# Class 0 of a dilated neighbourhood attention kernel: two half steps of eight rows in place of one step of sixteen

## The chip, the cores and the metric

The kernel runs on one core of a Trainium2 chip. The metric is the device time of one execution in microseconds (us). The core has five engines that run their own instruction queues in order: TensorE (PE in the profile, with its weight loads as PEld), VectorE (DVE), ScalarE (ACT), GpSimd (POOL) and SyncE (SP, which here only issues transfers). They meet at semaphores.

## What is computed

The input is an image of 224 x 224 pixels with 192 channels. Every pixel attends to 7 x 7 pixels around it, taken two apart, so a pixel sees only pixels of one row parity and one column parity. At the border the window is moved inwards, not cut.

```python
qkv = x @ wqkv                       # q, k, v of 192 channels each, one head
r0 = clip(ir - 6, 0, 223 - 12)       # first row of the window; columns likewise
ri = r0[:, None] + 2 * arange(7)     # its seven rows
logits = einsum('bnc,bnkc->bnk', q, k[window]) * 192 ** -0.5
o = einsum('bnk,bnkc->bnc', softmax(logits), v[window]) @ wo
```

## The kernel before

**Row classes.** Rows are put in two classes by the parity of the rows that they look at: class 0 looks at even rows, class 1 at odd ones. Each class has 112 query rows `v`. Class 0 holds the image rows 1, 3, 5 (moved in at the top border) and then 0, 2, 4, ...; class 1 holds 7, 9, ..., 223 and then 218, 220, 222. Query row `v` of class 0 needs the key rows `v-6` to `v` of its class (clipped at 0); row `v` of class 1 needs `v` to `v+6`. Columns are classed and shifted in the same way (`cc` 0 and 1), in 14 slots of 8 columns.

**Bands.** The image is loaded transposed (channels on partitions) in 14 bands of 16 image rows, eight rows of each class. A band is three transposing loads on the SP queue: channels 0 to 127 of the even columns to `XA[0]`, of the odd ones to `XA[1]`, and a middle part to `X1[b]` (two buffers). `xb_items` copies the middle part into `XB` (two copies of 64 x 1792 a band), and `sort_items` puts 8 x 8 pixel blocks next to one another in `XS` (three copies a band and class). Both run on POOL, those of the first bands on DVE. `XA` and `XB` hold six bands. The other 64 partitions of `XB` hold one-hot marks for row and column, which mask keys that lie outside a query's window; `marks` and `marks_on` spread them over the bands.

**Steps, pairs, jobs.** A step is 16 query rows of one class; the 14 steps take the classes in turn (`steps`). A job is one slot of a step: 16 rows x 8 columns = 128 queries. In TensorE the two row halves of a job (`h`) stand side by side, each with 64 weight columns. Two jobs make a pair, so a step is seven pairs. For pair `k` the loop issues `stage1` (scores, row maximum on DVE as `nmx`) and `stage1b` (exp on ACT as `p`); for pair `k-1` `stage2` (transposes of `p`, copied to `pt_sb`); for pair `k-2` `stage3` (`o_ps`) and `stage4` (division by the row sum, and the output transfers). Class 0's rows 0 to 7 have only eight key rows; in step 0 `key_rows` fills their window up with six masked ones.

**Work for the next step.** During a step, the pieces of the next one are made between the pairs (`w128`, `w64`). `g_items` gives the queries multiplied by the folded weights, in four groups of slots with three items each: two `whole` items, and one `halves` item that goes from PSUM to `gx` on ACT and then to `G` in two copies on POOL. `v_item` gives the values of one block of 16 key rows (`pv`, then `VF`); `vd_low` and `vd_high` copy halves of `VF` to `VD`, so that a row half finds its 16 key rows there in order. Step 0 makes its own values as well as those of step 1.

**Order.** `in_order` ties every engine to the program's order, so each queue is the order in which the Python code issues. POOL's copies go through a list, `pool_q`, of which up to four entries are issued after each pair. It also carries the output transfers of slot 0 (10 to 20 small ones per step), because the border columns go to odd places.

```python
steps = [(ti, rc) for ti in range(7) for rc in range(2)]
J.p = PP[J.rc][J.k % 2]
add = {0: sort_items(1, 1, pool), 1: sort_items(2, 1, pool), 3: sort_items(2, 0, pool), 5: xb_items(3, pool) + sort_items(3, 0, pool)}.get(m, [])
pool_q[:0] = add
pool_do(4)
```

Of the kernel before, what the change touches and what calls it, by code (L numbers as in the profile page):

```python
# [22 lines left out]
NSTEP = 14  # L23
# [33 lines left out]
def _rows(rc, ti):  # L57

    return [_phys(rc, 16 * ti + j) for j in range(16)]


def _runs8(rc, ti, h):

    return [(j0, nj) for (j0, nj, _r, _s) in _aff_runs(_rows(rc, ti)[8 * h:8 * h + 8])]
# [34 lines left out]
def kernel(  # L99
# [42 lines left out]
    for t in SS:  # L142
        nc.vector.memset(_win(t, 0, 128, 0, [[256, 2], [16, 14], [1, 2]]), NEG)

    def load_items(b):

        src = xp[16 * b:16 * b + 16].rearrange("r j c -> (r j) c")
        at = (16 * b) % (2 * RP) * S

        def one(k):  # L150
            if k == 1:
                X1[b] = x1_p.tile([128, BND], BF, name=f"x1_{b}", tag="x1")
            dst = X1[b][:] if k == 1 else XA[k // 2][:, at:at + BND]
            nc.sync.dma_start_transpose(out=dst.unsqueeze(1), in_=src[:, 128 * k:128 * k + 128])

        return [lambda k=k: one(k) for k in ((0, 2, 1) if b in (0, 2, 3) else (1, 0, 2))]
# [10 lines left out]
    def sort_items(b, rc, eng):  # L167

        hf = (b + rc) % 2
        return [lambda k=k: eng(out=_win(XS[rc], 0, 128, k * NSLOT * 128 + 64 * hf, [[128, NSLOT], [8, 8], [1, 8]]), in_=strip_in(b, rc, k))  # L170
                for k in (0, 2, 1)]
# [69 lines left out]
    for m in range(2):  # L241
        marks(m, 0, MM, nc.vector.tensor_copy)
    marks(0, MM, 2 * MM, nc.vector.tensor_copy)
# [3 lines left out]

    def g_col(rc, ti, s0, ns, eng):
        for cc in range(2):
            p = XCOL[cc]  # L250
            if s0 == 0:
                for h in range(2):
                    for (j0, nj) in _runs8(rc, ti, h):
# [4 lines left out]
    def g_row(rc, ti, s0, ns, eng, parts):  # L258

        for cc in range(2):  # L260
            p = XROW[cc]
            for (j0, nj, e0, estep) in parts:
                if s0 == 0:
                    for h in range(2):
                        for (r0, nr) in _runs8(rc, ti, h):
# [20 lines left out]
    g_col(0, 0, 0, 1, nc.scalar.copy)  # L286
# [14 lines left out]
    for rc in range(2):  # L301
        for t in PP[rc]:
            nc.gpsimd.memset(_win(t, 0, 128, 112 * rc, [[128, 8], [1, 16]]), 0.0)
# [32 lines left out]
    def v_mms(pv, at):  # L336
        for cc in range(2):
            for pas in range(2):
                for h in range(2):
# [17 lines left out]

    def v_first(j):
        def emit(dve):
            pv = ps_g.tile([128, 512], F32, name="pv", tag="pg")  # L360
            v_mms(pv, lambda k, h: _win(XS[1], 0, 128, k * NSLOT * 128 + 128 * j + 64 * h, [[1, 64]]))
# [3 lines left out]
    def first_sort(eng):  # L365
        return [lambda k=k: eng(out=_win(XS[1], 0, 128, k * NSLOT * 128, [[64, NSLOT], [8, 8], [1, 8]]), in_=strip_in(0, 1, k)) for k in (0, 2, 1)]  # L366
# [6 lines left out]
    def row_runs(rc, ti):  # L373

        runs = []
        for j, p in enumerate(_rows(rc, ti)):
# [23 lines left out]

    def g_items(rc, ti, s0, ns):
        rows = row_runs(rc, ti)
        w = 8 * ns

# [18 lines left out]
        def put(dst, off, pg, dve, p0=0, pn=128):  # L423

            a, m = s0, ns
            if s0 == 0:
                rr = [_runs8(rc, ti, h) for h in range(2)]
                if len(rr[0]) == len(rr[1]):
                    evac(_win(dst, p0, pn, off, [[64, 2], [8, 8], [1, 8]]), _win(pg, p0, pn, 0, [[8 * w, 2], [1, 8], [w, 8]]), dve)
                else:  # L430
                    for h in range(2):
# [3 lines left out]
            evac(_win(dst, p0, pn, off + (a - s0) * 128, [[8, 16], [128, m], [1, 8]]), _win(pg, p0, pn, 8 * (a - s0), [[w, 16], [8, m], [1, 8]]), dve)  # L435
# [8 lines left out]
        def halves(dve, direct=False):  # L444
# [9 lines left out]
            for cc in range(2):  # L454
                p = XDAT[cc]
                nc.gpsimd.tensor_copy(out=G[rc][cc][p:p + 64, 1, s0:s0 + ns, :], in_=gx[p:p + 64, 0:ns * 128].rearrange("p (s q) -> p s q", q=128))  # L456

        return [whole(0), whole(1), halves]

# [4 lines left out]
    def key_rows(J, h):  # L464

        i = 2 * J.ti + h
        if J.rc == 0:
            if i == 0:
                return [(MM - 6, 0, 6), (0, 6, 8)]
            v0 = 8 * i - 6  # L470
        else:
            v0 = 8 * i
        return [(v, v - v0, n) for (v, n) in _wraps(v0, 14)]

    def stage1(J, ab):
        s = 2 * J.m + ab
        s_ps = SS[ab]


        cols = {0: [(1, 7, S - 7), (8, 8, 0)], 2: [(1, 15, 9)]}.get(s, [(2, 14, 8 * s - 6)])  # L480
        lo = cols[0][0]
        for cc in range(2):
            units = []
            for h in range(2):
                u = []
                for (v, k0, n) in key_rows(J, h):
                    for (q, nq, c) in cols:
                        o = _win(s_ps, 64 * h, 64, cc * 256 + 16 * k0 + q, [[16, n], [1, nq]])
# [10 lines left out]
        nc.vector.tensor_reduce(out=nmx[:], in_=_win(s_ps, 0, 128, lo, [[256, 2], [16, 14], [1, 16 - lo]]), axis=AX.XY, op=ALU.max, negate=True)  # L499
        J.p = PP[J.rc][J.k % 2]  # L500
        J.s[ab] = (s_ps, nmx)

    def stage1b(J, ab):
        s_ps, nmx = J.s[ab]
        z = 16 if J.rc == 0 else 0
        for cc in range(2):
            nc.scalar.activation(out=J.p[:, ab, cc, :, z:z + 112].rearrange("p q (r k) -> p q r k", k=8), in_=_win(s_ps, 0, 128, cc * 256, [[8, 2], [16, 14], [1, 8]]),  # L507
                                 func=ACTF.Exp, bias=nmx[:, cc:cc + 1], scale=1.0)

    def stage2(J):  # L510
        J.pt = work.tile([128, 8, 128], BF, name="pt_sb", tag="pt_sb")
        if J.k == NP - 1:

            for ab in range(2):
                pt_ps = ps_g.tile([128, 4, 128], BF, name="pt_ps", tag="pg")
                for i in range(4):
                    for h in range(2):
                        nc.tensor.transpose(pt_ps[64 * h:64 * h + 64, i, :], J.p[:, ab, i // 2, i % 2, 64 * h:64 * h + 64], ident[:])
                nc.vector.tensor_copy(out=J.pt[:, 4 * ab:4 * ab + 4, :], in_=pt_ps[:])
            return  # L520
        pt_ps = ps_t.tile([128, 8, 128], BF, name="pt_ps", tag="pt")
        for ab in range(2):
            for cc in range(2):
                for q in range(2):
                    for h in range(2):
                        nc.tensor.transpose(pt_ps[64 * h:64 * h + 64, 4 * ab + 2 * cc + q, :], J.p[:, ab, cc, q, 64 * h:64 * h + 64], ident[:])  # L526
        (nc.scalar.copy if J.n == NSTEP - 1 and J.m < 5 else nc.vector.tensor_copy)(out=J.pt[:], in_=pt_ps[:])  # L527

    def stage3(J, ab):
        rc, s = J.rc, 2 * J.m + ab  # L530
        o_ps = (ps_o if J.k < NP - 1 else ps_g).tile([128, 512], F32, name="o_ps", tag="o" if J.k < NP - 1 else "pg")
        V = (VD[rc], VF[rc])
        for cc in range(2):
            for q in range(2):
                for h in range(2):
                    nc.tensor.matmul(o_ps[64 * h:64 * h + 64, cc * 193:cc * 193 + 193], lhsT=J.pt[:, 4 * ab + 2 * cc + q, 64 * h:64 * h + 64],  # L536
                                     rhs=V[h][:, (s - 1 + q) % NSLOT, cc * C:cc * C + 193], start=(q == 0), stop=(q == 1))
# [7 lines left out]
    def stage4(J, ab):  # L545
        rc, ti, s, o_ps = J.rc, J.ti, 2 * J.m + ab, J.o_ps[ab]
        rs = J.rs.get(ab) or stage4a(J, ab)
        if s > 0 and J.n == NSTEP - 1:

            o_sb = _win(XS[0], 0, 128, 2 * C * s, [[C, 2], [1, C]])  # L550
# [4 lines left out]
        if J.k >= NP - 3 and ab == 1:  # L555
# [5 lines left out]
        prow = _rows(rc, ti)  # L561
        if s > 0:
            for (j0, nj, r0, rstep) in _aff_runs(prow):
                def put(eng, j0=j0, nj=nj, r0=r0, rstep=rstep):
                    eng.dma_start(out=op[r0: r0 + (nj - 1) * rstep + 1: rstep, 8 * s - 3:8 * s + 5, :],
                                  in_=o_sb[8 * j0:8 * (j0 + nj)].rearrange("p t c -> p (t c)"))

                if J.n < NSTEP - 1:
                    put(nc.gpsimd if nj < 8 and s % 2 == 1 else nc.sync)
                elif nj >= 8:  # L570
                    put(nc.sync)
                elif s in SHORT:

                    for j in range(nj):
                        def row(eng, p=8 * (j0 + j), r=r0 + j * rstep, a=SHORT[s]):
                            eng.dma_start(out=op[r, 8 * a - 3:8 * s + 5, :].rearrange("(t i) c -> i t c", i=8),
                                          in_=_win(XS[0], p, 8, 2 * C * a, [[2 * C, s + 1 - a], [1, 2 * C]]))
                        if s < NSLOT - 1:
                            row(nc.gpsimd)
                        else:  # L580
                            end_q.append(row)
            return
        for h in range(2):
            for (j0, nj, r0, rstep) in _aff_runs(prow[8 * h:8 * h + 8]):
                for (cc, i0, n, mem, pair) in ((0, 0, 3, 1, 0), (0, 3, 5, 0, 0), (1, 6, 2, 1, 3), (1, 0, 3, 1, 109), (1, 3, 3, 0, 109)):
                    p = 64 * h + 8 * j0 + i0 * nj
                    dst = op[r0: r0 + (nj - 1) * rstep + 1: rstep, pair:pair + n, mem * C:(mem + 1) * C]
                    pool_q.append(lambda dst=dst, p=p, m=n * nj, cc=cc: nc.gpsimd.dma_start(out=dst.rearrange("j i c -> i j c"), in_=o_sb[p:p + m, cc, :]))  # L588

    steps = [(ti, rc) for ti in range(7) for rc in range(2)]  # L590
    pairs = []
    for n, (ti, rc) in enumerate(steps):
        for m in range(7):
            J = Pair()
            J.n, J.ti, J.rc, J.m, J.k, J.o_ps, J.s, J.rs = n, ti, rc, m, len(pairs), {}, {}, {}
# [3 lines left out]
    def g_all(n):  # L599
        ti, rc = steps[n]  # L600
        its = [g_items(rc, ti, s0, ns) for (s0, ns) in GROUPS]
# [4 lines left out]
    end_q = []  # L606
    SHORT = {7: 1, NSLOT - 1: 8}
# [4 lines left out]


    first0, first1 = ((0, 6, 0, 0), (6, 10, 0, 1)), ((0, 16, 0, 1),)
    g_row(0, 0, 0, 1, pool, first0)
    g_col(0, 0, 1, 3, pool)
# [159 lines left out]
```

## Time and profile before

| what | value |
|---|---|
| median of 3 runs | 362.85 us (362.56 to 364.27) |
| profiled execution, its own time | 360.51 us |
| its span | 358.7 us |
| busy PE, DVE, ACT, POOL | 93%, 88%, 86%, 79% of the span |
| step 0, first exp to first exp of step 1 | 37.46 us |
| step 1; step 2 | 23.37 us; 24.46 us |
| steps 3 to 12 | 226.64 us, 22.7 each |
| step 13 and what follows | 25.20 us |

The profiled execution is 2.34 us below the median. The steps are told apart by the first exp (`p`) of each, of which there are 28 a step. [...]

### The profile page before, as it was taken

To read this page: it belongs to the slowest core of one execution; us is meant where nothing else is said; L and a number is where in the kernel's file an instruction comes from. 1 tells how busy PE (TensorE), PEld (TensorE's weight loads), DVE (VectorE), ACT (ScalarE), POOL (GpSimd) and SP (SyncE) were. 2 spreads that over 40 slices of the span, in tenths; PEclk is the share of its full clock that TensorE was granted. 3 is DMA by queue.
4 is the path that set the end of the run, shared out by engine and by line. 5 is a ranking of instruction groups with operands and counts; after the bars stand their busy time and mean duration, and the time that the engine had idled before them with its cause. 6 is when DMAs were issued, how large, how long until landed. Compare 5 with 4: busy or idle time off the path is not lost.

```text
span 358.7 us, 19454 instructions
## 1 busy us (share of the span) xinstructions
PE 333.6 (93%) x8120; PEld 307.1 (86%) x8120; DVE 314.2 (88%) x744; ACT 308.2 (86%) x824; POOL 282.6 (79%) x445
## 2 busy tenths in 40 slices
PE   4788888998999999999999999999999999999872
PEld 2777777997999999999989999999999999999762
DVE  8967987897898998989989999899998989989893
ACT  6354777997999999999999999999999989999893
POOL 8966799999896996959969699596996878374182
PEclk9999999999999999999999999999999999999998
DMA  9999876799968979889898997999989965635423
GB/s 191 214 189 182 161 168 160 152 206 154 209 158 201 189 177 184 185 187 195 182 191 178 203 194 170 188 196 187 193 182 187 179 143 123 142 98 116 107 68 90
DMA packets 137539, 60.79 MB, mean 169 GB/s; under 512 B 88578, under 2 KB 136927, under 8 KB 137452
## 3 DMA queue, kind: packets, MB, share of 16 engines
q1 hardware_dynamic: 130052, 56.32, 78.5%
q0 software_dynamic: 5280, 1.71, 2.7%
q10 hardware_dynamic: 2120, 1.54, 2.3%
q8 instruction: 63, 1.03, 1.2%
q14 instruction: 24, 0.20, 0.2%
HBM read 0.29 MB, written 19.27 MB: 55 GB/s over the span
## 4 chain that ended last, share of the span: by engine, by line
PE 74%; DVE 10%; POOL 7%; ACT 5%; issue 2%; DMA 1%; DVEq 0%; SPq 0%; POOLq 0%; ACTq 0%
PE pv L341 17%; PE s L497 16%; PE o_ps L536 15%; PE pg L421 11%; PE pt_ps L526 10%; PE pgh L421 6%; ACT p L507 3%; POOL out_dram L588 2%; POOL xs L170 2%; DVE xb L160 2%; DVE nmx L499 2%; DVE g L329 1%; POOL xb L160 1%; POOL g L456 1%; ACT pt_sb L527 1%
## 5 line engine op out<-in xcount | busy, mean ns | idle before, releaser
L507 ACT ACTIVATE p<-s,nmx 128x224 bf16<-128x224 f32 x392 | 150.1, 450 | 25.7 <-DVE nmx L499 24.2
L499 DVE TENSOR_REDUCE nmx<-s 128x2 f32<-128x392 f32 (+1 forms) x196 | 102.5, 565 | 18.2 <-PE s L497 17.5
L456 POOL COPY g<-gx 64x512 bf16<-64x512 bf16 (+1 forms) x110 | 62.1, 564 | 52.7 <-ACT gx L331 45.8
L341 PE MATMUL pv<-wp,xs 128*64 128x192 bf16 x1624 | 93.1, 250 | 10.8 <-DVE xs L366 3.6
L341 PEld LDWEIGHTS <-xs 128*64 128x64 bf16 x1624 | 79.0, 112 | 24.0 <-issue 8.5
L559 DVE TENSOR_TENSOR o_sb<-o_ps,rs 128x384 bf16<-128x384 f32 x169 | 94.2, 558 | 5.9
L331 ACT CAST vf<-pv 128x384 bf16<-128x384 f32 x193 | 87.8, 522 | 11.1 <-PE pv L341 11.1
L588 POOL DMA_DIRECT2D out_dram<-o_s x150 | 84.6, 571 | 9.0 <-DVE rs L542 7.8
L536 PE MATMUL o_ps<-vd,pt_sb 128*64 128x193 bf16 x784 | 81.6, 246 | 2.3 <-ACT pt_sb L527 2.1
L497 PE MATMUL s<-xa,g 128*64 128x196 bf16 (+7 forms) x990 | 82.3, 233 | 1.2 <-ACT p L507 0.3
L497 PE MATMUL s<-xb,g 128*64 128x196 bf16 (+7 forms) x990 | 82.0, 232 | 0.7 <-DVE g L329 0.4
L536 PE MATMUL o_ps<-vf,pt_sb 128*64 128x193 bf16 x784 | 81.6, 246 | 0.0
L497 PEld LDWEIGHTS <-g 128*64 128x64 bf16 x1980 | 77.8, 110 | 3.6 <-issue 2.0
L536 PEld LDWEIGHTS <-pt_sb 128*64 128x64 bf16 x1568 | 71.5, 109 | 3.8 <-ACT pt_sb L527 3.2
L527 DVE COPY pt_sb<-pt_ps 128x1024 bf16<-128x1024 bf16 x92 | 63.2, 687 | 6.0 <-PE pt_ps L526 0.8
L526 PE MATMUL pt_ps<-ident,p 128*64 128x128 bf16 x1552 | 63.7, 219 | 0.0
L526 PEld LDWEIGHTS <-p 128*64 128x64 bf16 x1552 | 57.1, 110 | 4.9
L331 ACT CAST g<-pg 128x512 bf16<-128x512 f32 (+4 forms) x136 | 57.6, 470 | 2.3 <-PE pg L421 2.3
L421 PEld LDWEIGHTS <-aw 128*64 128x64 bf16 x1320 | 54.7, 110 | 3.9 <-issue 0.6
L421 PE MATMUL pg<-xb,aw 128*64 128x512 bf16 (+9 forms) x440 | 54.1, 269 | 0.0
L421 PE MATMUL pg<-xa,aw 128*64 128x512 bf16 (+9 forms) x440 | 52.3, 270 | 0.0
L170 POOL COPY xs<-xa 128x896 bf16<-128x896 bf16 x50 | 45.2, 930 | 1.4
(73 smaller groups left out, 283.9 us busy)
## 6 DMA issues: line engine op xcount, KB each, us to landing
vd<-vf SPq DMA_DIRECT2D x49, 336.9 KB
out_dram<-o_sb SPq DMA_DIRECT2D x156, 96.0 KB
out_dram<-o_s POOLq DMA_DIRECT2D x78, 9.0 KB, 3.9
out_dram<-o_sb SPq DMA_DIRECT2D x13, 78.0 KB
out_dram<-xs SPq DMA_DIRECT2D x13, 78.0 KB
vd<-vf SPq DMA_DIRECT2D x2, 337.8 KB
vd<-vf ACTq DMA_DIRECT2D x2, 336.9 KB
xa<-in_x_dram SPq DMA_TRANSPOSE x28
```

The source lines that it names most:

```text
L331: nc.scalar.copy(out=out_, in_=in_)
L341: nc.tensor.matmul(pv[64 * h:64 * h + 64, cc * C:(cc + 1) * C], lhsT=at(k, h), rhs=WP[(cc, pas)][:], start=(pas == 0), stop=(pas == 1))
L421: nc.tensor.matmul(o, lhsT=l, rhs=r, start=(pas == 0), stop=(pas == 1))
L456: nc.gpsimd.tensor_copy(out=G[rc][cc][p:p + 64, 1, s0:s0 + ns, :], in_=gx[p:p + 64, 0:ns * 128].rearrange("p (s q) -> p s q", q=128))
L497: nc.tensor.matmul(o, lhsT=w, rhs=r, start=(pas == 0), stop=(pas == 1))
L499: nc.vector.tensor_reduce(out=nmx[:], in_=_win(s_ps, 0, 128, lo, [[256, 2], [16, 14], [1, 16 - lo]]), axis=AX.XY, op=ALU.max, negate=True)
L507: nc.scalar.activation(out=J.p[:, ab, cc, :, z:z + 112].rearrange("p q (r k) -> p q r k", k=8), in_=_win(s_ps, 0, 128, cc * 256, [[8, 2], ...
L526: nc.tensor.transpose(pt_ps[64 * h:64 * h + 64, 4 * ab + 2 * cc + q, :], J.p[:, ab, cc, q, 64 * h:64 * h + 64], ident[:])
L527: (nc.scalar.copy if J.n == NSTEP - 1 and J.m < 5 else nc.vector.tensor_copy)(out=J.pt[:], in_=pt_ps[:])
L536: nc.tensor.matmul(o_ps[64 * h:64 * h + 64, cc * 193:cc * 193 + 193], lhsT=J.pt[:, 4 * ab + 2 * cc + q, 64 * h:64 * h + 64], rhs=V[h][:, ( ...
L559: nc.vector.tensor_tensor(out=o_sb[:], in0=_win(o_ps, 0, 128, 0, [[194, 2], [1, C]]), in1=rs[:].unsqueeze(2).to_broadcast([128, 2, C]), op ...
L588: pool_q.append(lambda dst=dst, p=p, m=n * nj, cc=cc: nc.gpsimd.dma_start(out=dst.rearrange("j i c -> i j c"), in_=o_sb[p:p + m, cc, :]))
```

## The change

`Step` objects take the place of `steps`. There are now 15 steps: class 0's rows 0 to 7 as a half step, then class 1 and class 0 in turn by sixteens (class 0 from row 8 on), and class 0's rows 104 to 111 as a half step at the end. A job of a half step holds two slots, `s` and `s+7`, of the same eight rows, where a job of a full step holds two row halves of one slot. A half step so has seven jobs in four pairs, the last of one job.

With that:

- The first half step has eight key rows per query, so `nk` is 8 and the scores and exps are 8 x 14 and 8 x 16 wide. It needs band 0 alone. Its values (`v_zero`, 14 items) go straight to both halves of `VD[0]`. Its `G` is made in two groups of seven slots.
- Both classes now use the bands 2t to 2t+2 in their step t. Step 1 is what step 0 was in its side work: it makes the values of its own (`v0`) and of step 2 (`vs`).
- The last half step's new values (`v_last`, 14 items) are four matmuls each on one side of the array, straight to `VD[0]`; its `G` items are half as wide.
- In the set-up, DVE clears the whole score buffers, and POOL clears more of `p`. DVE sorts band 0 for class 0 (`first_sort(0)`); POOL sorts it for class 1, copies the marks of step 0's `G` in full, and takes `xb_items(1)`. ACT takes the marks of step 1's first slots.
- During step 1 POOL's list is longer: both sorts of class 0 for bands 1 and 2, the marks of rows 16 to 34 (`even_marks`, `odd_marks`, `marks`), `xb_items(3)`, `xb_items(4)`, the sorts of bands 3 and 4 for class 1, the marks of step 2's `G` over all slots, step 0's ten slot-0 transfers (`edge_q`) and step 1's.
- The output of the first half step is kept in a part of `XA[1]` that band 4 takes later, and written out by 16 transfers on SP during step 1 (`row_q`, four a pair). Band 4's load is held back to the fourth pair of step 1 and after. The output of the last half step is kept in `XS[1]` and issued on SP, POOL and, for the last one, ACT. The single-row transfers at the end (`SHORT`, `end_q`) are gone.

```diff
-    for t in SS:
-        nc.vector.memset(_win(t, 0, 128, 0, [[256, 2], [16, 14], [1, 2]]), NEG)
+        nc.vector.memset(t[:], NEG)
...
+STEPS = [Step(0, 0, 0, 8)]
+for _t in range(7):
+    STEPS.append(Step(len(STEPS), 1, 16 * _t, 16))
+    STEPS.append(Step(len(STEPS), 0, 16 * _t + 8, 16 if _t < 6 else 8))
...
+    def v_zero(cb):
+        def emit(dve):
+            pv = ps_g.tile([128, 512], F32, name="pv", tag="pg")
+            v_mms(pv, lambda k, h: first_block(0, k, cb))
+            evac(_win(VD[0], 0, 128, cb * VP, [[193, 2], [1, C]]), pv[:, 0:2 * C].rearrange("p (t c) -> p t c", c=C), dve)
+        return emit
+    def v_last(cb):
+        def emit(dve):
+            pv = ps_g.tile([128, 512], F32, name="pv", tag="pg")
+            v_mms(pv, lambda k, h: XS[0][:, k, cb, 0:64], (1,))
+            evac(_win(VD[0], 64, 64, cb * VP, [[193, 2], [1, C]]), pv[64:128, 0:2 * C].rearrange("p (t c) -> p t c", c=C), dve)
+        return emit
...
     def stage1(J, ab):
-        s = 2 * J.m + ab
-        s_ps = SS[ab]
+        s_ps, st = SS[ab], J.st
+        nk, lo = (8 if J.n == 0 else 14), 2
+            for half, (s, h) in enumerate(J.jobs[ab]):
...
+    for st in STEPS:
+        for mm in range(4 if st.half else 7):
+            J.jobs = [((s, 0), (s + 7, 0) if st.half else (s, 1)) for s in (2 * mm, 2 * mm + 1) if not st.half or s < 7]
...
+            if n == 0:
+                w128 = (vz[4:10], vz[10:] + vf1[:2], vf1[2:], gw[0:2])[m]
+            elif n == 1:
                 w128 = (v0[:9] + gw0[2:4], v0[9:] + gw0[4:6], gw0[6:8] + vs[0:3], gw[0:2] + vs[3:6], gw[2:4] + vs[6:9], gw[4:6] + vs[9:12], gw[6:8] + vs[12:])[m]
             elif n + 1 < NSTEP:
-                w128 = gw[m + (m > 1):m + 1 + (m > 0)] + vs[2 * m:2 * m + 2]
+                v_at = (0, 0, 0, 3, 6, 9, 12, 14) if n + 2 == NSTEP else (0, 0, 2, 4, 6, 8, 11, 14) if n == 2 else range(0, 16, 2)
+                w128 = gw[m + (m > 1):m + 1 + (m > 0)] + vs[v_at[m]:v_at[m + 1]]
...
-        if ld:
+        if ld and (n != 1 or m > 2):
             ld.pop(0)()
...
+        elif n == 1:
+            for _ in range(4):
+                if row_q:
+                    row_q.pop(0)(nc.sync)
+            add = {0: sort_items(1, 0, pool), 1: sort_items(2, 0, pool), 2: [lambda q=q: even_marks(q, pool) for q in range(2)], 3: xb_items(3, pool),
+                   4: [lambda q=q: odd_marks(q, MM + 6, 2 * MM, pool) for q in range(2)] + [lambda q=q: marks(q, 2 * MM, 2 * MM + 3, pool) for q in range(2)],
+                   5: sort_items(3, 1, pool), 6: xb_items(4, pool) + sort_items(4, 1, pool)}[m]
...
+            g_row(STEPS[2], 1, 13, pool, ((0, 16, 2, 1),))
...
-        pool_do(4)
+        pool_do(max(4, len(add)) if n < 2 else 4)
+        if n == 1:
+            for _ in range(min(2, len(edge_q))):
+                edge_q.pop(0)()
```

## The prediction

> **What bounds the kernel now.** I read the busy time by step first (span from-to, then length, and busy time and count of PE, PEld, DVE, ACT, POOL, clock, DMA share, GB/s), cut at the first exp of steps 0, 1, 2, 3 and 13.
>
> ```profile
> 10.54:21.57 11.03, 9.53 (x195) 8.95 (x197) 10.57 (x24) 4.47 (x15) 8.92 (x15) 1.00 1.20 214
> 21.57:59.03 37.46, 32.15 (x714) 26.72 (x712) 28.92 (x61) 25.00 (x62) 30.00 (x42) 1.00 0.90 171
> 59.03:82.40 23.37, 22.60 (x528) 20.67 (x525) 20.59 (x50) 21.33 (x57) 22.68 (x40) 1.00 0.80 169
> 82.40:106.86 24.46, 22.99 (x528) 20.71 (x525) 20.63 (x50) 21.45 (x58) 23.10 (x33) 1.00 0.97 178
> 106.86:333.50 226.64, 226.46 (x5796) 214.26 (x5793) 206.14 (x491) 213.04 (x576) 178.06 (x265) 1.00 0.86 174
> 333.50:358.70 25.20, 15.86 (x359) 13.29 (x353) 18.22 (x50) 16.96 (x39) 10.36 (x18) 0.93 0.38 90
> ```
>
> Steps 3 to 12 are TensorE's: 22.7 us each at a full clock, PE busy all the time. Steps 1 and 2 are not quite: there POOL is the engine with next to no gap (22.68 of 23.37). So what happens before about 86 us is decided by POOL, after it by PE. The chain that ended last says the same, and the waits from 58 to 92 us (what waited, on what: us, times, longest) show where POOL's work is handed over:
>
> ```profile
> 79.45 1.68 POOL xb L160
> 81.17 1.69 POOL xb L160
> 82.92 2.69 POOL xs L170 x3
> 85.66 0.68 PE pv L341 x11
> ...
> PE pv L341 <- POOL xs L170: 1.9, 3, 0.7
> PE pgh L421 <- POOL xb L160: 0.2, 1, 0.2
> ```
>
> From 58 to 86 us that chain lies on POOL almost alone. Its two ends matter: band 4's `XB` copies end at 82.9 and let step 2 make the first `G` of step 3 (pgh, which starts at 82.91); the sorts of band 4 end at 85.6 and let it make step 3's first values (pv). The prices (busy us, mean ns):
>
> ```profile
> L588 POOL DMA_DIRECT2D out_dram<-o_s x150 | 84.6, 571 | 9.0 <-DVE rs L542 7.8 <-issue 1.1
> L456 POOL COPY g<-gx 64x512 bf16<-64x512 bf16 x84 | 51.7, 615 | 48.8 <-ACT gx L331 43.2 <-issue 3.1
> L456 POOL COPY g<-gx 64x256 bf16<-64x256 bf16 x26 | 10.4, 399 | 3.9 <-ACT gx L331 2.6
> L170 POOL COPY xs<-xa 128x896 bf16<-128x896 bf16 x50 | 45.2, 930 | 1.4
> L160 POOL COPY xb<-x 64x1792 bf16<-64x1792 bf16 x22 | 36.9, 1679 | 1.7 <-DMA x<-in_x_dram 0.6
> L233 POOL COPY xb<-xb 64x672 bf16<-64x672 bf16 x2 | 1.5, 743 | 0.1
> L271 POOL COPY g<-e 32x728 bf16<-32x728 bf16 x2 | 1.6, 788 | 0.1
> L268 POOL COPY g<-e 32x64 bf16<-32x64 bf16 x12 | 3.7, 325 | 0.3
> ```
>
> **The change, part by part.** I follow three points: when POOL may start step 1's list, when it has band 4 in `XB`, and how much is left from there.
>
> *1. The first half step.* DVE's queue loses three mark copies ahead of its first sort (0.75 + 0.75 + 1.28 us), and gains full clears of the two score buffers (the old ones of 56 elements take 0.17 together; 512 elements at the 0.5 to 1 ns of nearby rows: 0.9 for both, ends 0.4 and 1.1) and two marks of 336 elements (0.2 each, from 0.75 at 1792). Sorts now begin at 8.8 (10.4 before), `XB`'s band 0 is there at 12.0 (sorts 2 x 0.45, copies 0.71 and 1.58 as measured). PE can start the first `G` item at 10.8 and ACT empties it from 11.3. From there I sum ACT's queue: eight `G` copies 2.9 and a wait of 1.2 for the second half of `XB`, four value copies at 0.49, ten mark copies at about 0.18 (six take 0.96 at the start): first exp at 19.4 (21.57 before). The half step has 14 exps of 128 columns (0.37 apiece in a row at 224; 0.28 taken), 13 value copies at 0.49, three divided outputs at 0.73, four `G` copies at 0.29: 13.6. Step 1's first two exps and `gx` take 1.35. Without a gap that is 34.3. In the first 60 us of before ACT waited 9.3 us for maxima in 8 waits; the half step has seven such places with the same shallow pipeline, so I add 2.6: POOL's first `gx` copy of step 1 starts at **36.9** (34 to 40). POOL has done its set-up and both sorts of the bands 1 and 2 by about 26 and idles until then, as it idled 8 us in step 0 before; so the work moved to it ahead of step 1 costs nothing.
>
> *2. POOL's list in step 1, up to band 4's `XB`.* In its order of issue: 7 pairs of `gx` copies (6 x 1.27 + 0.85 = 8.5), three sorts (3 x 2.74 = 8.2; a sort is 1.81 + 0.93), `XB` of bands 3 and 4 (6.8), `even_marks` (two of 1792 elements, 3.4), `odd_marks` (two of 1120: 1.1 each from 0.74 at 672 and 1.68 at 1792), `marks` 1.5, the marks of step 2's `G` (8 x 0.22, and two of 1664 elements at 1.55 from 0.79 at 728: 4.9), 15 transfers at 0.57 (8.5). Sum 44.0. The same prices summed over before's list, from 22.96 to 82.87, give 54.3; it took 59.9 with 5.0 idle, so the sum is good to 1 us. None of these copies should wait: the loads of bands 3 and 4 are issued behind freed buffers, some 15 us ahead of use. Band 4 is in `XB` at 36.9 + 44.0 = **80.9** (77 to 85), against 82.9 before: 2.0 us sooner, where half a step of work has been skipped.
>
> PE gets there earlier. Step 1 has 31 us of PE work (a step's 22.5, 14 more value items at 0.34, nine more `G` items at 0.43), ACT and DVE have 31 and 32, and step 0 of before, with the same side work on an empty pipeline, took 37.5. So PE stands at step 2's first pgh between 66 and 73, and waits 8 to 14 us. Queued behind that pgh is all that PE has (transposes, `G`, the next scores), so DVE and ACT run dry too. Values at step 2 come a pair later (`v_at`), by when the sorts (80.9 + 2.7) are done: the 2.0 us that pv waits in before are saved.
>
> *3. What is left from there.* Before: from pgh at 82.9 to the first exp of step 13 at 333.5, 250.6; without pv's waits 248.6. Steps 2 to 12 hold the same items after the change, and wrap at the same number of places. So step 13 starts at **329.5**.
> Before, 25.2 us were left; now there is a full step with side work, and a half step. Step 13: scores, transposes and outputs as ever; `G` items of half width (2.7 instead of 5.2 us); the values 14 x 0.34 as ever. By pairs: two without values at DVE's 2.9 (as the last step's pairs), five at 2.7 to 3.3: 21.4 (20 to 22.5). The half step has three pairs at the last step's mean of 2.6 and then one of one job: 8.0 to its exp. From the last pair's exp to the end before took 9.7; one job instead of two saves about 1.3, the one transfer at the end instead of a queue of rows about 0.8: 7.6 (6.5 to 9.5). Sum **37.0** (34.5 to 40).
>
> [...] Each item has 4 matmuls instead of 8. Eight take 0.34 us (16 in 0.68 in the chain), and one alone, from the durations at 512 and 96 columns (392 and 208 ns, 0.44 ns a column), takes 84 ns: 4 alone are 0.34 too. [...] By count alone 2.4 us would be saved in step 13, and the time would come out that much lower. [...]
>
> The other edits: 14 more value items (4.7 us of PE) lie in the half step and step 1, where PE waits anyway; with that cover gone they cost 4.7. Step 0's narrow scores save about 1 us of PE there, for nothing. The 16 row transfers on SP lie beside step 1. SP stands at band 3's `X1` until POOL has sorted band 1 (41 us), and at band 4's `XA[1]` until `edge_q`'s transfers have landed (71.6 + 3.9), so that load lands near 80 (a transposing load took 3.5 to 5 us from issue): about when `XB` is ready. Taken at nothing; up to 3 us if it is late.
>
> **Sum.** 80.9 + 248.6 + 37.0 = 366.5 of span, 7.8 over 358.7. The profiled execution then has 368.3 for its 360.51; on the median of 362.85 it is **370.6 us**. The sum of the ends goes from 361 to 373 of span.
>
> **Rivals.**
> - *POOL does not hold (faster).* If band 4 is ready when PE asks at about 70, the front saves 11 more: 70 + 248.6 + 37.0 = 355.6, or 359.7 on the median. For it: the first scores do come 4 us sooner, and the front of before has 6 us of gaps in step 0. Against it: POOL's 44.0 us are all in one queue behind step 1's first `gx`. It decides once band 4 is ready before 73.1: then the front pays for the 11.8 us of the longer end. That asks for 8 us less on POOL. Chance 0.14.
> - *About even.* Band 4 at 71 to 75: 361.0 to 364.7. Start at 34, list of 40. Chance 0.10.
> - *Mildly slower.* The end costs only 34.5 and POOL is 2 us early: 366. Counted at 364.7 to 366: 0.06.
> - *Worse.* `XA[1]` of band 4 lands 3 us after `XB`, and the half step takes 3 us more: 376. Chance 0.08.
> - The forecast, 366 to 375: 0.62.
>
> **Chances.** Under 0.5% (1.8 us) this kernel's runs tell no change. Faster 0.14, same 0.10, slower 0.76. The range 361 to 375 leaves out most of the faster case and the worse one, about 0.2.
>
> **What would show it.** Right: the first exp near 19.4, that of step 1 near 35.5; POOL with no gap from 37 to past 90; PE idle for 8 us or more before a pgh that waits on POOL's `xb` near 81; steps 3 to 12 at 22.5; step 13 near 21.4 and 15.6 after it. Wrong: a wait below 3 us there, or on a transfer; a POOL list that starts before 33; or steps 2 to 12 above 23.

## The result, and the profile after

The changed kernel takes **418.79 us** (median of 6 runs, 417.56 to 419.67) against 362.98 us for the kernel before on the same chip (362.39 to 364.27): a ratio of **1.153**, 95% interval 1.150 to 1.156. I had predicted 370.6 us with a range of 361 to 375. The direction was right. The size was not: the loss is 56 us where I had priced 8, and the time lies far outside the range. The profiled execution has a span of 416.9 us (358.7 before, 366.5 in my sum) and a mean granted clock of 0.953 (0.995 before).

As before, I read the busy time by step first. The stretches are cut at the first exp of step 0, 1, 2, 3, 13 and of the last half step. Each row has its length, the busy time and the count of PE, PEld, DVE, ACT and POOL, then the granted clock (on record from 26 us on), the DMA share and GB/s:

```profile
0.00:31.81 31.81, 13.74 (x228) 11.84 (x229) 26.56 (x38) 12.43 (x44) 24.74 (x41) 1.00 0.75 138
31.81:48.60 16.79, 12.53 (x294) 11.87 (x295) 10.20 (x27) 11.44 (x36) 2.00 (x3) 0.90 0.44 86
48.60:104.77 56.17, 36.66 (x659) 29.97 (x654) 28.75 (x65) 26.06 (x65) 38.79 (x55) 0.85 0.43 86
104.77:143.09 38.32, 25.45 (x518) 22.98 (x515) 20.87 (x49) 21.62 (x58) 28.39 (x38) 0.86 0.79 161
143.09:375.97 232.88, 229.17 (x5807) 218.16 (x5804) 206.59 (x491) 212.82 (x577) 178.78 (x266) 0.99 0.82 167
375.97:398.50 22.53, 21.20 (x470) 19.79 (x466) 20.16 (x50) 19.07 (x58) 13.98 (x28) 1.00 0.44 104
398.50:416.90 18.40, 8.67 (x188) 6.87 (x184) 10.62 (x29) 8.45 (x20) 7.64 (x14) 0.87 0.25 67
```

The loss sits in the first 143 us. In the set-up (first row) DVE and POOL are both busy nearly all the time, DVE for 26.6 us of 31.8. In step 1 (third row) no engine is: 56.2 us, of which the busiest, POOL, works 38.8 and PE 36.7. Step 2 takes 38.3 us for PE work of 25.4. From step 3 on the machine runs as it did, PE-bound, at 23.3 us a step against 22.7.

Against the span of my sum, point by point:

| point | forecast | measured | added |
|---|---|---|---|
| first exp of step 1 | 35.5 | 48.6 | +13.1 |
| step 2's first pgh | 80.9 | 110.4 | +16.4 more |
| first exp of step 13 | 329.5 | 376.0 | +17.0 more |
| end | 366.5 | 416.9 | +3.9 more |

*The set-up.* Timeline of DVE, then of POOL, then PE's first `G` matmul (start, us in all, engine, line, operation, how many; in brackets the idle time ahead and its releaser):

```profile
15.51 2.81 DVE L635 COPY xb<-xb 64x336 bf16<-64x336 bf16 x2
18.83 4.11 DVE L169 COPY xb<-x 64x1792 bf16<-64x1792 bf16 x2
...
15.06 3.13 POOL L635 COPY xb<-xb 64x1456 bf16<-64x1456 bf16 x2
18.14 4.33 POOL L169 COPY xb<-x 64x1792 bf16<-64x1792 bf16 x2
...
23.00 0.22 PE L451 MATMUL pg<-xb,aw 128*64 128x9 bf16 x2 [11.18 <-DVE xb L169]
```

Two DVE copies of 336 elements, for which I had 0.2 us each, take 1.4 us each: about as long as POOL's copies of 1456 elements that run at the same time. The two `XB` copies take 2.06 us each. DVE shows no idle time there: the time lost is inside its instructions. PE waits 11.2 us for the second `XB` copy, the one that I had ready at 12.0 us, and the first exp comes at 31.8 instead of 19.4.

*Step 1.* The chain that ended last, at the first pair of step 1 and then at the end of that step (start, us, what):

```profile
52.17 1.81 POOL xs L179 x2
...
54.00 1.42 SPq L163
...
55.53 0.69 SPq L384
...
56.27 5.62 DMA vd<-vf
...
103.86 1.98 DMA out_dram<-xa
...
106.16 4.10 DMA xa<-in_x_dram
```

and the longest waits between 30 and 135 us, then one from 135 to 376 us (what waited, on what: us, times, longest):

```profile
POOL g L486 <- ACT gx L342: 31.3, 3, 15.2
ACT vf L342 <- DMA vd<-vf: 10.8, 1, 10.8
PE pgh L451 <- DMA xa<-in_x_dram: 5.4, 1, 5.4
...
PE s L524 <- DMA xb<-xb: 7.0, 1, 7.0
```

This is read from the ACT line backwards. ACT, about to empty step 1's values into `VF[1]`, stands 10.8 us until `first_vd`, which reads the same slots, has landed. `first_vd` was issued at 55.5 us; ACT had emptied the last of its slots by 44.4. It was queued on SP behind band 3's transposing load of `X1`, and that waited for an `X1` buffer, hence for POOL's sort of band 1, which POOL only begins after step 1's first `gx`. While ACT stands, PE gets no free PSUM, the next `gx` is not made, and POOL, whose list I had called the bound, idles for 15.0 us after the first 5 of it. At the end of step 1 band 4's load into `XA[1]` goes out behind the half step's last output row, which landed at 105.8 us, and PE waits 5.4 us for it at step 2's first pgh; POOL's `XB` had been ready 1.2 us before. The last line is step 3's: its first scores wait for `marks_on`, which the change had moved from step 0 to step 2.

### The profile page after: what moved, and what is told of

Same layout as the page of the kernel before. It is cut to its first block, busy times and chain, and to the rows that moved or that the text cites. A ratio compares the mean times of both kernels' runs of the same rounds, so it can differ in the third digit from the quotient of the medians.

```text
span 416.9 us, 19491 instructions
## 1 busy us (share of the span) xinstructions
PE 347.4 (83%) x8134; PEld 321.5 (77%) x8134; DVE 323.8 (78%) x745; ACT 311.9 (75%) x853; POOL 294.3 (71%) x442
## 4 chain that ended last, share of the span: by engine, by line
PE 59%; POOL 11%; DMA 9%; issue 7%; ACT 6%; DVE 3%; SPq 2%; POOLq 0%; ACTq 0%; DVEq 0%
PE pv L352 13%; PE s L524 13%; PE o_ps L553 12%; PE pg L451 9%; PE pt_ps L543 8%; DMA vd<-vf 6%; PE pgh L451 5%; ACT p L534 4%; POOL xs L179 2%; DMA xa<-in_x_dram 2%; POOL g L278 1%; POOL out_dram L581 1%; DVE nmx L526 1%; POOL out_dram L609 1%; DMA xb<-xb 1%
## 5 line engine op out<-in xcount | busy, mean ns | idle before, releaser
L534 ACT ACTIVATE p<-s,nmx 128x224 bf16<-128x224 f32 (+1 forms) x392 | 148.9, 448 | 34.2 <-DVE nmx L526 33.0
L526 DVE TENSOR_REDUCE nmx<-s 128x2 f32<-128x392 f32 (+2 forms) x196 | 101.8, 559 | 34.5 <-PE s L524 33.3
L486 POOL COPY g<-gx 64x512 bf16<-64x512 bf16 (+2 forms) x110 | 60.2, 547 | 96.0 <-ACT gx L342 92.1
L352 PE MATMUL pv<-wp,xs 128*64 128x192 bf16 x1680 | 99.8, 250 | 25.4 <-ACT vf L342 13.5
L524 PE MATMUL s<-xb,g 128*64 128x196 bf16 (+6 forms) x960 | 84.5, 236 | 7.1 <-DMA xb<-xb 7.0
L524 PEld LDWEIGHTS <-g 128*64 128x64 bf16 x1920 | 80.1, 112 | 12.4 <-issue 9.3
L524 PE MATMUL s<-xa,g 128*64 128x196 bf16 (+6 forms) x960 | 85.4, 237 | 2.4 <-ACT g L342 1.2
L451 PEld LDWEIGHTS <-aw 128*64 128x64 bf16 x1338 | 66.8, 115 | 23.4 <-issue 20.8
L544 DVE COPY pt_sb<-pt_ps 128x1024 bf16<-128x1024 bf16 (+1 forms) x97 | 66.1, 681 | 17.6 <-PE pt_ps L543 12.4
L342 ACT CAST g<-pg 128x512 bf16<-128x512 f32 (+5 forms) x138 | 57.3, 460 | 16.3 <-PE pg L451 16.2
L451 PE MATMUL pg<-xb,aw 128*64 128x512 bf16 (+18 forms) x446 | 57.3, 276 | 11.2 <-DVE xb L169 11.2
L451 PE MATMUL pg<-xa,aw 128*64 128x512 bf16 (+18 forms) x446 | 58.9, 277 | 0.1
```

The costliest lines, as they stand in the source:

```text
L342: nc.scalar.copy(out=out_, in_=in_)
L352: nc.tensor.matmul(pv[64 * h:64 * h + 64, cc * C:(cc + 1) * C], lhsT=at(k, h), rhs=WP[(cc, pas)][:], start=(pas == 0), stop=(pas == 1))
L451: nc.tensor.matmul(o, lhsT=l, rhs=r, start=(pas == 0), stop=(pas == 1))
L524: nc.tensor.matmul(o, lhsT=w, rhs=r, start=(pas == 0), stop=(pas == 1))
L534: nc.scalar.activation(out=J.p[:, ab, cc, :, z:z + 8 * nk].rearrange("p q (r k) -> p q r k", k=8), in_=_win(s_ps, 0, 128, cc * 256, [[8, 2 ...
L544: (nc.scalar.copy if J.n == NSTEP - 1 and J.m < 2 else nc.vector.tensor_copy)(out=J.pt[:, 0:nj, :], in_=pt_ps[:, 0:nj, :])
```

## The experiments

My theory after the result: the work was priced about right, and three separate places on one path hold it up, (1) the order of two issues on SP, (2) the late `marks_on`, (3) POOL's copies beside DVE's in the set-up. The rivals: POOL's list sets step 2 whatever lies ahead of it, as I had predicted, so that removing a wait gains nothing; or a removed wait is replaced by the next. Three runs undo one place each, the fourth all three. The runs were made in three sets: in those of the first four, the next three and the last two, the kernel before took 363.0, 362.3 and 363.5 us, so times of different sets are comparable to about 1 us.

**One issue moved on SP.** In step 0, band 3's last load goes behind `first_vd`:

```
-        if ld and (n != 1 or m > 2):
+        if ld and (n != 1 or m > 2) and (n > 0 or m != 2):
```

> Only the place of one issue on SP changes: band 3's transposing load of X1 goes behind the two transfers of first_vd instead of ahead of them. Theory (SP's order): first_vd is then issued at about 50 us, when its last evacuation is done, instead of 55.5; it lands near 54-56 instead of 62.0, ACT's wait on vd<-vf falls from 10.8 us to 2-5 us, the first pair of step 1 from 20.3 us to 10-14 us, POOL's 15 us wait for the second gx shortens by as much, and the whole kernel comes to 406-412 us. Rival A (the wait lies beside POOL's list, which sets step 2 anyway): step 2's first pgh stays at 109-111 us and the time at 416-419 us. Rival B (the wait moves): the transfers of vd are as late for another reason (bandwidth, another semaphore), ACT still waits 9-11 us for vd<-vf, 416-419 us.

Measured 404.76 us: 14.0 below the changed kernel, and 1.2 below the lower end of what theory gave. SP's timeline:

```profile
43.41 1.38 SPq L384 DMA_DIRECT2D vd<-vf  x2
53.00 1.76 SPq L163 DMA_TRANSPOSE x<-in_x_dram  x1
```

`first_vd` goes out at 43.4 us instead of 55.5, the wait of ACT on `vd<-vf` is gone from step 1, and the first pair takes 7.9 us instead of 20.3. The load of band 3 is issued at 53.0, as late as before, and nobody misses it. The order of two issues cost some 14 us (12.5 of the 13.1 us by which the span is shorter lie in step 1); both rivals fall.

**`marks_on` earlier.**

```
-        if n == 2 and m >= 3:
+        if n == 1 and m >= 3:
             marks_on(m % 2, 2 * MM + 3 + (m - 3) // 2)
```

> marks_on is issued in step 1's last four pairs instead of step 2's. Theory: the last of its four transfers lands before 110 us instead of at 141.5, the 7.0 us wait of step 3's scores on xb<-xb is gone, and with it the half clock of 139-145.8 us; step 2's last pair falls from 11.8 us to 4-5 us and the kernel to 408-412 us. Rival A (the transfers' work only moves: 2.9 MB more to carry beside step 1's, where SP already queues): what step 2 gains step 1 loses, the first pgh of step 2 comes 3-8 us later than 110.4, and the time stays at 414-420 us. Rival B (step 3 waits next for something as late, such as its own pgh or vd): under 2 us gained, 416-419 us.

Measured 407.70 us, 11.1 below the changed kernel. Step 2's last pair falls from 11.8 to 4.3 us and step 3 from 24.1 to 22.4; the first pgh of step 2 comes no later (108.8 us). Of the 11.7 us by which the span is shorter, 8.2 lie in these two steps and 0.6 behind them. The other 2.9 were gained in the set-up, the half step and step 1, where I know of no reason for it; so I put the price of the late `marks_on` at 8 to 11 us. Its four transfers carry 0.73 MB, not the 2.9 that I had written.

**Seven set-up copies from POOL to ACT.** DVE keeps its own list unchanged:

```
-    for it in first_sort(1, pool):            # behind the first values
-    for q in range(2): odd_marks(q, 3, MM, pool)
+    for it in first_sort(1, act) + xb_items(1, act):   # ahead of the first G items
+    for q in range(2): odd_marks(q, 3, MM, act)
-                pool_q += xb_items(1, pool)            # step 0
```

and POOL sorts band 2 ahead of band 1 in step 0.

> POOL's seven set-up copies of 128x896, 64x1456 and 64x1792 between 10.2 and 22.5 us go to ACT, which stands idle from 10.6 to 24.1 us; POOL's sort of band 2 goes ahead of that of band 1, so that POOL copies nothing beside DVE's last 8 us before the first G matmul. DVE keeps exactly its own copies. Theory (DVE and POOL hold each other up whenever both copy in SBUF): DVE's 64x1792 copies fall from 2.06 us each to under 1 us, its odd marks from 1.4 us to under 0.4 us, the first G matmul goes from 23.0 us to 15-18 us, the first exp from 31.8 to 23-27 us, everything behind moves with it, and the kernel comes to 408-413 us. Rival A (DVE waits for the transposed loads or its copies are that long by themselves): the durations stay within 15%, the first exp stays at 30-33 us, 416-420 us. Rival B (the wait moves to ACT, which now has some 9 us of copies in front of the weights' evacuations it owes to PE): first exp at 29-33 us with ACT as the releaser, 415-420 us.

Timeline of DVE in that run, then of ACT:

```profile
13.16 0.57 DVE L635 COPY xb<-xb 64x336 bf16<-64x336 bf16 x2
...
14.25 1.25 DVE L169 COPY xb<-x 64x1792 bf16<-64x1792 bf16 x2
...
13.10 3.38 ACT L169 COPY xb<-x 64x1792 bf16<-64x1792 bf16 x2
```

With ACT copying the same tiles at the same time, DVE's instructions take 0.29 and 0.63 us instead of 1.40 and 2.06. The cause is shown: it was POOL's copying, not the copies and not the loads. The first `G` matmul goes from 23.0 to 15.6 us and the first exp from 31.8 to 25.5 us, inside what theory gave. The whole comes to 414.45 us, 4.3 less, where I had written 408 to 413: in the trace 2.5 us of the 6.3 are lost again behind, 1.8 of them in steps 3 to 12, and why was not tried. The waits of step 1 are as in the changed kernel (ACT stands 10.7 us for `vd<-vf`).

**All three.**

> The three edits together. Theory (three separate losses of 11-16, 7-10 and 6-9 us on one path, with the work itself as I costed it): POOL's 44 us list in step 1 runs without a wait, step 2's first pgh comes at 80-88 us, and the kernel at 378-390 us: near the 370.6 us I had predicted, and still slower than before. Rival A (POOL's list or band 4's load sets step 2's start whatever is ahead of it): the gains don't add, pgh of step 2 at 98 us or later and the kernel at 395-412 us. Rival B (the extra work never cost anything, all of the loss was these three waits): within 3 us of the kernel before, 360-366 us.

Measured 391.27 us (ratio 1.075, interval 1.067 to 1.082): 27.5 below the changed kernel, where the three single gains add to 29.5. So they are separate losses on one path. It is 1.3 us above theory's upper end, and the reason is in the trace. POOL's list now starts at 44.4 us and runs with one wait of 2.6; its copies of band 4 are done at 91.4 us. That is 44.4 us of list, against my 44.0. But pgh comes at 93.8, and what PE waits for is not POOL (waits from 86 to 96 us):

```profile
PE pgh L451 <- DMA xa<-in_x_dram: 6.7, 1, 6.7
```

**Which of the two holds step 2: three more runs on top of the last.** In the first run, the half step's outputs are kept in band 5's place of `XA`, so that band 4 can be loaded at once:

```
-            home, at = (XA[1], 2 * MM * RW) if J.n == 0 else (XS[1], 0)
+            home, at = (XA[1 - s // 4], 5 * BND + 2 * C * (s % 4)) if J.n == 0 else (XS[1], 2 * C * s)
```

As it ran, it left out the last two of the 32 output row transfers that this needs. In the second, POOL's copies of marks in step 1 go to DVE (`even_marks`, `odd_marks`, `marks`: `pool` becomes `dve`). The third has both, and leaves out the same two transfers.

> On top of e4_all_three: the half step's outputs are kept in band 5's place of XA (four slots in XA[1], three in XA[0]) instead of band 4's, so band 4's loads are issued in step 1's first three pairs and wait for no output; the output rows become 32 transfers of three or four slots, five per pair, instead of 16. In e4_all_three step 2's first pgh came at 93.7 us, 2.2 us after POOL had copied band 4 into XB (91.4). Theory (POOL's list stands right behind the transfer): pgh goes to 91-92 us and the time falls by 1.5-3 us, to 388-390 us. Rival A (band 4's load was the only late thing): pgh at 84-88 us, 380-386 us. Rival B (16 more issues on SP, 0.35 us each, push SP's other transfers back): 391-395 us.

> On top of e4_all_three: POOL's copies of marks in step 1 (even marks 3.4 us, odd marks 2.3 us, marks 1.5 us; 7.2 us in all) go to DVE, which spends about 3.3 us on them. Band 4's load into XA[1] stays behind the half step's output rows. Theory (two limits within 2.2 us of each other, the transfer the later one): POOL is done some 7 us earlier, pgh still waits for XA[1] until 92-94 us, and the time stays within 2 us of 391.3. Rival (POOL's list alone sets step 2, as I had predicted): pgh at 85-88 us, 383-386 us.

> e5_home_moved and e6_pool_lighter together. Theory (POOL's list sets step 2 once no transfer is late): pgh at 83-87 us and the time at 381-385 us, that is 5-8 us below e5_home_moved for 7.2 us taken off POOL's list. Rival A (the pairs of step 1 themselves take that long: PE, ACT and DVE are what is left): pgh at 89-92 us, 387-391 us. Rival B (DVE's extra copies and POOL's hold each other up, and give back what POOL saves): 386-390 us with DVE's copies of 64x1792 above 1.2 us each.

Measured 387.91, 392.22 and 385.78 us (ratios 1.071, 1.083 and 1.066). What PE's first pgh of step 2 waits for, in this order (the third from the timeline):

```profile
PE pgh L451 <- POOL xb L169: 5.4, 1, 5.4
```

```profile
PE pgh L451 <- DMA xa<-in_x_dram: 7.7, 1, 7.7
```

```profile
87.63 0.22 PE L451 MATMUL pgh<-xb,aw 128*64 128x48 bf16 x2 [1.59 <-POOL xb L169]
```

The first two came out as theory had them. With the load early, PE waits on POOL, at 90.8 us, as I had predicted for the change itself. With POOL lighter but the load late, nothing is gained: band 4 is in `XB` at 86.6 us instead of 91.4, and pgh waits for `XA[1]` until 93.0.

The third brought 2.1 us, not 5 to 8 (4.2 us between the two profiled executions). PE still waits on POOL there, at 87.6 us. What fell short is how much lighter POOL became. `pool_do(4)` issues up to four entries after each pair, and where the marks are gone it takes output transfers that stood further back. POOL's timeline in the run with the load early, then in the one with both:

```profile
62.99 3.40 POOL L640 COPY xb<-xb 64x1792 bf16<-64x1792 bf16 x2
```

```profile
63.88 2.34 POOL L609 DMA_DIRECT2D out_dram<-o_s  x4
...
75.31 2.40 POOL L609 DMA_DIRECT2D out_dram<-o_s  x4
```

Ahead of band 4's `XB` there are now 20 transfers instead of 15, and the list up to there takes 43.2 us instead of 46.9, 2.6 us of waiting in each: 3.7 us less, not 7.2. Over the whole of step 1 POOL is as busy as before. Here is step 1 by itself (from its first exp, same columns as above), first with the load early, then with both:

```profile
42.49:85.09 42.60, 33.33 (x659) 27.21 (x655) 28.81 (x65) 25.97 (x65) 37.61 (x53) 1.00 0.59 120
```

```profile
43.07:85.74 42.67, 33.90 (x659) 27.16 (x654) 32.39 (x71) 25.75 (x64) 37.61 (x56) 1.00 0.61 122
```

So the bound is theory's, and the time between theory's and that of rival A (step 1's own pairs). PE reaches pgh at 86.0 us, only 1.6 us before POOL is done, so by then the two are near level. What sets the pairs up to there was not tried. POOL's 37.6 us are one candidate. Another is the marks on DVE: ACT waits 10.1 us for row maxima in step 1, against 5.6 in the run with the load early. DVE and POOL did not hold each other up much inside the instructions: DVE's two copies of 1792 elements take 0.88 us each, under the 1.2 set as the sign.

**All rows, and the tail.** The next run has both edits with the row transfers complete; the last one then takes four transfers of the last half step from POOL:

```
-            for (u, p, eng) in ((s, 0, nc.sync), (s2, 64, nc.gpsimd if J.m < 3 else nc.scalar)):
+            for (u, p, eng) in ((s, 0, nc.sync), (s2, 64, nc.gpsimd if J.m < 1 else nc.sync if J.m < 3 else nc.scalar)):
```

> e7_both with the half step's row transfers issued six per pair instead of five: they start only in step 1's second pair, so five per pair sent 30 of the 32, and e5_home_moved and e7_both left out the last two (three slots each of two rows); here all go out. Theory: two issues of 0.35 us off the path, the time is that of e7_both, 384-387 us, with step 2's first pgh at 87-89 us. Rival (SP was at its limit in step 1, and six per pair push its other transfers back): 388-392 us, with a wait of PE or ACT on vd or xa in step 1.

> On top of e8_both_all_rows: of the last half step's outputs of slots 7 to 13, those of its second and third pair go out on SP instead of POOL. In the trace of after, POOL issues 12 transfers of 0.57 us without a gap from 405.5 to 411.8 us, 0.4 us after the last copy of an output, and the span ends 5.1 us after the last of them. Theory (POOL's issues end the span): 4 issues fewer on POOL, the last POOL issue 2.3 us earlier, the time 1-2.5 us below e8_both_all_rows. Rival (the last output's own copy and its transfer end the span, SP and ACT are as late as POOL): within 0.7 us of e8_both_all_rows, or above it where SP's issues now come last.

Measured 387.61 us (ratio 1.068, interval 1.063 to 1.072) and 388.31 us (1.069, 1.065 to 1.074). The first is the fastest version that writes everything, and still 24 us behind the kernel before. The time lies above the 384 to 387 expected and short of the rival's 388; by the ratios, 1.066 and 1.068, it can't be told from that of the run with 30 row transfers. Step 2's first pgh comes at 88.4 us, as expected. The trace has the rival's sign: step 2's transfer of `vd` is issued at 92.2 us, behind six row transfers (88.3 with five a pair), and PE waits 2.4 us for it in step 2's third pair, which takes 7.4 us instead of 3.4. The tail theory fell. POOL's last issue ends 2.6 us earlier (380.1 instead of 382.7 us) and the stretch from the last half step's first exp to the end shrinks only from 18.4 to 17.8 us, while the time does not fall. The rival's sign is there: SP's last issue now ends at 384.3 us (383.0 before), later than POOL's did. What ends the span is left open.

## Why the prediction was wrong, step by step

**The price of the work was right.** Measured from the first `gx` copy to the end of band 4's `XB`, POOL's list took 59.3 us in the changed kernel, 15.0 of them waiting: 44.3 us against my 44.0. The run with the load early shows the predicted bound, PE waiting for POOL's `XB` at step 2's first pgh. The first half step (16.8 us, of which 16.1 were forecast) and the pairs of the last one (7.9 against 8.0) are right too, and so is the value item of the last half step (`v_last`, 4 matmuls instead of 8): the four start 82 ns apart while each lasts 0.24 us, 0.33 us an item. An item of eight in step 1, at 80.2 us, has its starts 40 ns apart and takes 0.33 us too.

**Part 1 of the prediction failed at one sentence**, "so the work moved to it ahead of step 1 costs nothing". I had asked only whether POOL was free, not whom its copies would slow. The set-up was 12.4 us later than forecast. 6.3 of these came back when the copies went to ACT. The trace of that run shows where the rest is. Its first `G` matmul is 4.8 us later than forecast: ahead of DVE's mark copies, between 2.8 and 9.1 us, four small instructions (128x128 and 128x16) take 1.75, 1.50, 1.50 and 0.81 us, beside POOL's wider clears of `p` and its marks of `G`, where the kernel before has 0.28, 0.18, 0.18 and 0.41. That is 4.5 us. From the first `G` matmul to the first exp it takes 10.0 us for my 8.6, as ACT is busy with the copies until 19.2 us. No run took these two away.

The sign had been in the trace of the kernel before. Of DVE's four equal copies of 64x1792 there, my sum took over the first two as measured, 0.71 and 1.58, without asking why they differ. Here are the second and the last; POOL was copying 32x1280 from 12.0 to 15.1 us:

```profile
12.43 1.58 DVE xb L160
...
15.62 0.62 DVE xb L160
```

The runs of the change show the same for `XB`'s band 0: 2.06 us a copy beside POOL's copies, 0.63 beside ACT's. Through what the two hold each other up, no run shows.

**Part 2 failed at "None of these copies should wait", and at what I did with SP.** I had seen that "SP stands at band 3's `X1` until POOL has sorted band 1 (41 us)", and took it at nothing because the load itself is not urgent. That it isn't was confirmed. What I didn't ask is what is queued behind it: `first_vd`, two transfers that ACT's next evacuation must not overtake. From there the wait ran through ACT and PE to POOL. It cost 14.0 us, the largest single term. The "up to 3 us if it is late" for band 4's `XA[1]` was about right: with the other waits gone it was 2.4 us behind POOL, and moving it away brought pgh 3.0 us forward.

**The edit that I had not priced at all** is `marks_on`. Between its old place in step 0 and its first reader in step 3 lay two whole steps; from its new place in step 2 it lands at 141.5 us, 7.0 after step 3 needed it. The sentence on step 3 onwards, "Steps 2 to 12 hold the same items", counted items and not when they are due.

**The estimate of step 1 without POOL was not put to the test.** I let PE stand at pgh 31 to 37 us after step 1's first exp. In no run was it there before 42.9, but POOL worked 37.6 us or more of step 1 in all of them. So whether the rival "POOL does not hold", which asked for 8 us less on POOL, could have given 359.7 us stays open; 3.7 us less brought the end 2 to 4 us forward.

**The rest.** In the run with the load early pgh comes at 90.8 us for my 80.9: POOL's list starts 6.9 us late and waits 2.6. From pgh to step 13 it takes 254.8 us for my 248.6, and the end 41.0 for 37.0. Step 13 has 22.5 instead of 21.4, and from the last pair's exp to the end it is 10.5 us instead of 7.6. In the changed kernel steps 5, 8 and 9 are 1.0 to 1.8 us longer than in the one before, and ACT waits for `vd<-vf` in steps 5, 6 and 9 (3.2 us in all). Why these transfers land later than before, and what lengthens step 8, was not tried.

That the change loses was forecast for a reason that held: the end is longer. Between the kernel before and the version with all rows, the two profiled spans differ by 29.1 us. The end is 15.7 of them (11.8 forecast). The front, where I had a gain of 2.0, loses 5.5, and the stretch from pgh to step 13, where I also had a gain of 2.0, loses 7.9.

Of the signs by which it would show itself wrong, two came true: the wait at step 2's first pgh was "on a transfer", and steps 3 to 12 took 23.3 us each, "above 23".

## What to carry to other kernels

When a wait is known and harmless for the instruction that waits, price the next instruction in the same queue: one transposing load that nobody needed yet cost 14 us through the transfer behind it. For an edit that moves a transfer, compare its landing with the moment that its first reader stands there, even where the reader is two steps away. Where a queue is filled by number, taking entries off it lets later ones move up: 7.2 us of copies gone made it 3.7 us shorter. And work given to an idle POOL was not free here while DVE copied: look for the time inside DVE's instructions (the same copy at 0.63 and 2.06 us), not in its idle time.

## What the runs showed of the hardware

*A wait cost more than its length.* In the changed kernel the granted clock of TensorE was at half for 13.65 us around the 10.0 us for which PE waited in step 1, and for 6.83 us around each of the waits of 5.4 and 7.0 us. Busy time in the first of these stretches, then in one of the run with all three edits (granted clock is the figure before the DMA share):

```profile
53.66:67.31 13.65, 4.79 (x44) 3.43 (x43) 1.81 (x3) 2.48 (x6) 1.56 (x3) 0.50 0.55 111
```

```profile
62.80:69.63 6.83, 5.14 (x85) 5.00 (x81) 2.85 (x7) 2.82 (x9) 6.73 (x9) 0.50 0.09 21
```

The lengths of all four, one of 13.65 us and three of 6.83, are multiples of 3.41 us, the length of the two shortest stretches at half in the changed kernel (33.18 to 36.59 and 84.38 to 87.79). A long wait was not needed: around the last of the four PE's gaps, just ahead of it and in it, were 1.2, 1.5 and 1.7 us, all on POOL's copies (`xs`, then `XB`), with matmuls between them, and the clock was halved for 6.8 us all the same. Nor does the length of one gap decide it: in the run with the load early a gap of 2.85 us, up to 66.4 us, left the clock at full speed (1.00 over the whole of step 1), and in the changed kernel one of 2.85, up to 84.9 us, went with 3.41 us at half. What does decide it is not shown. Where the lighter POOL list cut the wait at pgh from 5.4 to 1.6 us, the clock stayed at full speed and the first two pairs of step 2 fell from 13.2 to 8.1 us: 5.1 us for 3.8 us less of waiting.

*POOL was slower too when it copied beside DVE*, but by little: its `XB` copies take 2.17 us each in the set-up of the changed kernel and 1.70 in step 1, while DVE's take 2.06 in that set-up and 0.62 behind it, at 41.6 us.
